# The mask of the first five attention pairs as a small matmul, with other due times for the planner

## The chip, the cores and the metric

One core of a Trainium2 chip runs the whole kernel. The metric is the device time of one execution in microseconds (us). Five engines work side by side: TensorE (PE; its weight loads have a row of their own, PEld), VectorE (DVE), ScalarE (ACT), GpSimd (POOL) and SyncE (SP), whose queue issues all of this kernel's transfers.

## What is computed

Block-causal attention for 4 batches, 8 heads, 576 positions and 64 channels a head, then two mixing blocks on its output:

```python
scores = scale * np.matmul(q, k.transpose(0, 1, 3, 2))
mask = pos[:, None] // 64 >= pos[None, :] // 64
scores = np.where(mask, scores, -1000000000.0)
attn = softmax(scores)                       # written out with max, exp, sum
x = np.matmul(attn, v)                       # heads side by side: 576 x 512 a batch
theta = x @ w_theta
zr, zi = x * np.cos(theta), x * np.sin(theta)
y = w_tok_r @ zr + w_tok_i @ zi              # over the 576 positions
u = x + y
x = u + np.maximum(u @ w_ch, 0.0)
u = x + low_rank_mix(x)                      # U, V of rank 32, over the positions
out = u + np.maximum(u @ w_ch1, 0.0) @ w_ch2 # 512 -> 2048 -> 512
```

Weights arrive as 64-bit floats and are decoded on the chip to a pair of 32-bit parts (high and low).

## The kernel before

The attention works on pairs of heads: 4 pairs a batch, 16 in all, numbered gp = 0 to 15. A pair has five row tiles of up to 128 positions (t = 0 to 4). `prep(gp)` loads q, k and v of a pair and scales q; `smax(gp, t)` makes the scores of a row tile and their softmax; `norm(gp)` takes the reciprocals of the row sums; `trans(gp, t, hh)` transposes the probabilities; `av(gp, part)` multiplies them by v (tiles oA and oB). One pair's `smax` calls are interleaved with the `trans` and `av` calls of the pair before.

In `smax` the two heads sit in the lower and upper 64 partitions of q and k, and write to the two banks of a score tile s. For t = 0 two blocks are made at once, one of 128 and one of 256 columns (the second is read by t = 1); t = 2 and 3 make 384 and 512 columns. Within a row tile the upper 64 rows must not see the last 64 columns. A DVE memset writes NEG = -1.0e30 there, behind the matmuls and ahead of the DVE reduction that takes the maximum (nm). ACT then takes the exponentials (P). t = 4 needs no mask.

`load_weight` brings one weight in two halves (raw_th, raw_tok, raw_ch) and `decode` turns them into high and low parts: two ACT activations and two DVE operations a half (da_th, da_tok, da_ch), then a rounding (on POOL, DVE or ACT) and a subtraction (on POOL or DVE). For each batch follow `theta` (five tiles), `sines` (once the five are there: one ACT table load, then the sines), `product` (five tiles), `mix_r`, `mix_i`, `chan`, `lowrank` and `expand`. The feed-forward (m and acc) runs over all batches at the end and begins earlier in gaps.

The order of the instructions is written by a planner in the kernel file. Each call is queued with a due time; the due times come from `CFG`, in units in which the four pairs of a batch take L = 60. Batch b's theta tiles are due from (b + 1) x 60 on, spread over T; the sines one after T, the products spread over P, then R and I for the mixing, twice X for the low-rank part. The weights of theta are due between d0 and d1 (as parts of 60), the first five token weights between d1 and d2, the others up to `dec`. `Line.run` lays out all operations by these due times, engine by engine, with a cost formula for each instruction. `Line.plan` repeats that four times with the latest possible starts of the layout before as the new due times, and keeps the round that it sees end first. Operations marked as `either` may go to any of two or three engines. `keep_warm` puts stand-in transposes (t<-ident, rb<-ident) into TensorE's planned gaps in the early part. All planned instructions are issued from one line, 1195.

Of the kernel before, what the change touches and what calls it, by code (L numbers as in the profile page):

```python
# [12 lines left out]
F32 = mybir.dt.float32  # L13
# [11 lines left out]
P = 128  # L25
# [10 lines left out]
NEG = -1.0e30  # L36
# [7 lines left out]


TC = {'schedule_with_timeline_sim': True}
CFG = dict(L=60., d0=0., d1=0.7, d2=1.0, dec=1.8, T=8.4, P=10., R=25.74, I=29.568, X=7., m0=4., m1=70., w1=1., w2=2., w3=0.2, wx=24., po=0.5)
ENG = dict(qs="p", pt00="a", pt01="d", pt20="a", pt21="d", pt30="a", pt31="d", pt40="a", pt41="d", pt5="d", oA="d", oB="d", nrm="p", xd="p", xh="p", zh="p", zl="p", uh="a", ul="p", sh="p", sl="p", dl="p", dh="a", os="p")
NR = 15
PA = 2  # L50
# [18 lines left out]
ROUNDS = 4  # L69
PATIENCE = 0.0  # L70
WARM = 140e3


class Op:
# [453 lines left out]
def build(tc, ctx, qT, kT, v, w_theta, wtokT, w_ch, U, V, w1, w2, outT):  # L528
    nc = tc.nc
    w_theta, wtokT, w_ch, U, V, w1, w2 = [a.bitcast(U32) for a in (w_theta, wtokT, w_ch, U, V, w1, w2)]  # L530
# [38 lines left out]
    const = ctx.enter_context(tc.tile_pool(name="const", bufs=1))  # L569
# [13 lines left out]
    warm = const.tile([P, 1], F32, name="warm")  # L583
    nc.scalar.activation(out=warm, in_=halfpi, func=AF.Exp)

    real = nc
    nc = line = Line(nc)
    pools = {"wk": ctx.enter_context(tc.tile_pool(name="wk", bufs=1)),
# [69 lines left out]
    def smax(gp, t):  # L658
        n = "%d_%d" % divmod(gp, NC4)
        if gp not in sx:  # L660
            sx[gp] = {a: line.tile([P, 9], F32, a, f"{a}{n}") for a in ("nm", "sm", "rs")}
            ptiles[gp] = {}
        x = sx[gp]
        nm, sm = x["nm"], x["sm"]
        q, k = qk[gp]
        if t != 1:
            x["s"] = line.tile([P, 2, 512], F32, "s0" if gp < 4 else "ss", f"s{n}_{t}", PSUM)
        s = x["s"]
        i = 2 * t
        if t < 4:  # L670
            W = P * (t + 1)
            src = s[:, :, 256:512] if t == 1 else s[:, :, :W]
            if t == 0:
                both = [(s[:, :, :P], 0, P), (s[:, :, 256:512], P, 2 * P)]
            elif t > 1:
                both = [(src, t * P, W)]
            if t != 1:
                line.together(lambda: [nc.tensor.matmul(y[:, hh], q[64 * hh:64 * hh + 64, c0:c0 + P],
                                                        k[64 * hh:64 * hh + 64, :w], start=True, stop=True)
                                       for y, c0, w in both for hh in range(2)])  # L680
                last = s.rearrange("p h (g c) -> p h g c", c=64)[0:64, :, 1::6] if t == 0 else src[0:64, :, W - 64:W]
                nc.vector.memset(last, NEG)
            pt = line.tile([P, 2, W], F32, f"P{t}", f"P{n}_{t}")
            nc.vector.tensor_reduce(out=nm[:, i:i + 2], in_=src, axis=AX.X, op=ALU.max, negate=True)
            for hh in range(2):
                nc.scalar.activation(out=pt[:, hh], in_=src[:, hh], func=AF.Exp, bias=nm[:, i + hh:i + hh + 1],
                                     scale=1.0, accum_out=sm[:, i + hh:i + hh + 1])
        else:
            for g in range(2):
                nc.tensor.matmul(s[:, g, :SH], q[:, 512:640], k[:, g * SH:(g + 1) * SH], start=True, stop=True)  # L690
            pt = line.tile([P, S], F32, "P4", f"P{n}_4")
            src = s[:, :, :SH]
            nc.vector.tensor_reduce(out=nm[:, i:i + 1], in_=src, axis=AX.XY, op=ALU.max, negate=True)
            nc.scalar.activation(out=pt.rearrange("p (g c) -> p g c", g=2), in_=src, func=AF.Exp,
                                 bias=nm[:, i:i + 1], scale=1.0, accum_out=sm[:, i:i + 1])
        ptiles[gp][t] = pt
# [252 lines left out]
    def at_time(t, fn, *args):  # L949
        units.append((t, len(units), fn, args))  # L950

    def spread(t0, t1, calls):
        for i, c in enumerate(calls):
            at_time(t0 + (t1 - t0) * i / len(calls), *c)
# [8 lines left out]
    def pair_calls(gp):  # L963
        calls = []
        for x in ORD.split():
            if x[0] == "S" and gp + 1 < NP:
                calls.append((smax, gp + 1, int(x[1])))
            elif x == "N" and gp + 1 < NP:
                calls.append((norm, gp + 1))
            elif x == "L" and gp + 2 < NP:  # L970
                calls.append((prep, gp + 2))
            elif x[0] == "T":
                calls.append((trans, gp, int(x[1])) + ((int(x[2]),) if len(x) > 2 else ()))
            elif x[0] == "A":
                calls.append((av, gp, int(x[1])))
        return calls

    for c in ((prep, 0),) + tuple((smax, 0, t) for t in range(NS)) + ((norm, 0), (prep, 1)):
        at_time(-1.0, *c)
    L = CFG["L"]  # L980
    for gp in range(NP):
        spread(gp * L / NC4, (gp + 1) * L / NC4, pair_calls(gp))
    d0, d1, d2, d3 = [L * CFG[x] for x in ("d0", "d1", "d2", "dec")]
    spread(d0, d1, [(load_weight, "th", w_theta, k, DM) for k in range(NC4)])
# [3 lines left out]
    for b in range(B):  # L988
        t0 = (b + 1) * L
        if b == B - 1:  # L990
            t0 += 1.0
        spread(t0, t0 + CFG["T"], [(theta, b, i) for i in range(NS)])
        t0 += CFG["T"]
        at_time(t0, sines, b)
        t0 += 1.0
        spread(t0, t0 + CFG["P"], [(product, b, i) for i in (4, 0, 1, 2, 3)])
        t0 += CFG["P"]
        spread(t0, t0 + CFG["R"], [(mix_r, b, g, d) for g in range(2) for d in range(NC4)])
# [18 lines left out]
    wx = []  # L1017
# [134 lines left out]
    def keep_warm(order):  # L1152
# [7 lines left out]
        for o in order:  # L1160
            if o.pe and o.start < WARM:
                free = [(-q[i][0], j, q[i][2]) for j, q in enumerate(homes.values()) for i in range(len(q))
# [78 lines left out]
```

## Time and profile before

| | |
|---|---|
| median of three runs | 861.77 us (859.32, 861.77, 861.82) |
| the profiled execution's own time | 861.41 us |
| its span, first to last instruction | 859.6 us |
| mean granted TensorE clock | 0.998 of full |
| busy share: PE, PEld, DVE, ACT, POOL | 98%, 80%, 48%, 44%, 31% |

The shares are means over the span. The stretches differ a lot: the first 60 us belong to the attention of batch 0 and to the weights, from about 60 to 505 us attention, mixing and the beginning of the feed-forward overlap, and from 505 us on there is only the feed-forward. A matmul's row counts its whole duration, and several may overlap; the weight loads' row is closer to how densely TensorE is fed.

### The profile page before, as it was taken

The numbers are of one execution on the slowest core, as the hardware profiler recorded it, in microseconds if no ns is written. First come the engines' busy times: TensorE is split into PE (matmuls) and PEld (weight loads), VectorE is DVE, ScalarE is ACT, GpSimd is POOL, SyncE is SP. The second block draws the span as 40 slices with busy tenths as digits, with TensorE's granted clock in tenths as the row PEclk, the third lists the DMA queues.
The fourth block names the chain that finished last, engine by engine and source line by source line (L and its number), as shares of the span: only waits on it lengthen the run. The fifth ranks groups of instructions, "written<-read, shape, count | busy, mean of one in ns | idle before, by whom it ended". The sixth has DMA issues, their size and how long they took to land.

```text
span 859.6 us, 12665 instructions
## 1 busy us (share of the span) xinstructions
PE 841.3 (98%) x4902; PEld 687.4 (80%) x4902; DVE 414.2 (48%) x793; ACT 374.4 (44%) x862; POOL 263.4 (31%) x286
## 2 busy tenths in 40 slices
PE   8999999999999999999999999999999999999998
PEld 6656688887888878988889778898888888888886
DVE  5997687467546575288756951512111311120112
ACT  6987977676556765359344641211101111111010
POOL 3546356534143431566253350404000500010000
PEclk9999999999999999999999999999999999999999
DMA  6652231110201102053423440402000100010001
GB/s 216 189 181 75 97 99 56 44 43 32 100 16 46 44 3 71 23 186 111 136 92 123 158 137 0 152 4 74 1 0 1 50 1 0 1 50 1 0 1 49
DMA packets 41595, 57.18 MB, mean 67 GB/s; under 512 B 4672, under 2 KB 25664, under 8 KB 41536
## 3 DMA queue, kind: packets, MB, share of 16 engines
q1 hardware_dynamic: 41536, 56.39, 20.1%
q8 instruction: 38, 0.62, 0.3%
q14 instruction: 21, 0.17, 0.1%
HBM read 46.94 MB, written 9.44 MB: 66 GB/s over the span
## 4 chain that ended last, share of the span: by engine, by line
PE 84%; DVE 6%; ACT 5%; DMA 2%; issue 1%; POOL 1%; SPq 0%; ACTq 0%; DVEq 0%; POOLq 0%
PE acc L1195 22%; PE m L1195 21%; PE y L1195 12%; PE c L1195 5%; PE th L1195 5%; PE s L1195 5%; PE t L1195 5%; PE oB L1195 4%; DVE d_w L1195 2%; DMA raw_w<-w 1%; ACT P L1195 1%; PE oA L1195 1%; PE xp L1195 1%; PE G L1195 1%; DMA raw_th<-w_theta 1%
## 5 line engine op out<-in xcount | busy, mean ns | idle before, releaser
L1195 PE MATMUL acc<-hh,w 128*128 128x512 f32 (+1 forms) x900 | 205.4, 373 | 1.1 <-ACT hh L1195 0.4
L1195 PE MATMUL m<-us,w 128*128 128x512 f32 (+1 forms) x900 | 203.1, 372 | 0.3 <-DVE w L1195 0.3
L1195 PEld LDWEIGHTS acc<-hh,w 128*128 128x128 f32 x900 | 156.6, 188 | 34.1 <-DVE o L1195 1.4
L1195 PEld LDWEIGHTS m<-us,w 128*128 128x128 f32 x900 | 156.8, 188 | 31.1 <-DVE w L1195 0.8
L1195 DVE SCALAR_TENSOR_TENSOR hh<-m,hh 128x512 fp32r<-128x512 f32 (+1 forms) x80 | 51.0, 637 | 266.2 <-ACT hh L1195 266.2
L1195 ACT ACTIVATE hh<-m 128x512 fp32r<-128x512 f32 (+1 forms) x80 | 44.4, 555 | 293.0 <-PE m L1195 288.0
L1195 PE MATMUL y<-wtok,zh 128*128 128x288 f32 x576 | 119.9, 301 | 0.1
L1195 PEld LDWEIGHTS y<-wtok,zh 128*128 128x128 f32 x576 | 92.6, 188 | 5.3 <-DVE xT L1195 2.4
L1195 ACT ACTIVATE P<-s,nm 128x128 f32<-128x128 f32 (+2 forms) x144 | 78.9, 552 | 40.8 <-DVE nm L1195 33.3
L1195 PE MATMUL y<-wtok,zl 128*128 128x288 f32 x288 | 85.0, 297 | 0.1
L1195 PE MATMUL t<-ident,P 128*128 128x128 f32 x400 | 64.5, 280 | 4.9 <-ACT PTB L1195 1.4
L1195 DVE TENSOR_REDUCE nm<-s 128x2 f32<-128x256 f32 (+4 forms) x80 | 64.3, 804 | 6.8 <-PE s L1195 3.4
L1195 PE MATMUL s<-k,q 64*128 64x128 f32 (+4 forms) x320 | 65.8, 459 | 0.0
L1195 PEld LDWEIGHTS t<-ident,P 128*128 128x128 f32 x400 | 47.9, 142 | 18.4 <-ACT P L1195 2.5
L1195 PE MATMUL c<-u,wch 128*128 128x288 f32 x384 | 60.3, 302 | 0.8 <-DVE u L1195 0.8
L1195 PEld LDWEIGHTS c<-u,wch 128*128 128x128 f32 x384 | 53.8, 188 | 5.5 <-issue 1.7
L1195 POOL TENSOR_TENSOR o<-us,us 128x512 f32<-128x512 f32 x16 | 20.7, 1320 | 115.4 <-DMA outT<-o 85.5
L1195 PEld LDWEIGHTS y<-wtok,zl 128*128 128x128 f32 x288 | 53.9, 188 | 1.7 <-POOL zl L1195 0.6
L1195 DVE TENSOR_TENSOR xT<-y,xT 128x288 f32<-128x288 f32 x64 | 29.0, 454 | 50.3 <-PE y L1195 49.6
L1195 PE MATMUL th<-wth,xh 128*128 128x512 f32 x160 | 51.9, 404 | 0.2 <-ACT xh L1195 0.2
L1195 ACT COPY PTB<-t 128x384 f32<-128x384 f32 (+3 forms) x68 | 30.4, 460 | 34.7 <-PE t L1195 33.6
L1195 POOL TENSOR_TENSOR zl<-f,zh 128x512 fp32r<-128x512 f32 x18 | 23.0, 1292 | 64.2 <-PE y L1195 61.4
(163 smaller groups left out, 1141.9 us busy)
## 6 DMA issues: line engine op xcount, KB each, us to landing
raw_w<-w SPq DMA_DIRECT2D x32, 512.0 KB, 4.0
raw_tok<-wtokT SPq DMA_DIRECT2D x18, 288.0 KB, 3.3
q<-qT SPq DMA_DIRECT2D x16, 320.0 KB, 2.9
vr<-v SPq DMA_DIRECT2D x16, 320.0 KB, 3.3
k<-kT SPq DMA_DIRECT2D x16, 288.0 KB, 3.3
u3d<-xT SPq DMA_DIRECT2D x16, 288.0 KB, 2.2
outT<-o SPq DMA_DIRECT2D x16, 256.0 KB, 2.1
raw_th<-w_theta SPq DMA_DIRECT2D x8, 256.0 KB, 5.4
```

Of the source, the lines that this page charges most:

```text
L1195: fn(*[place(x) for x in args], **{k: place(x) for k, x in kw.items()})
```

## The change

For gp < NMASK = 5, `smax` issues no memset. Instead, each group of score matmuls is followed by a mask product for each head into the last 64 columns of its block: a constant tile mrow, whose first row in each half has ones in columns 0 to 63, times a constant tile mneg, whose first row in each half is NEG. It is accumulated onto the scores (start=False). Six DVE memsets at the beginning build the two constants. Pairs 5 to 15 keep the memset. In `CFG` five due-time settings differ: d1 0.7 to 0.84, T 8.4 to 13.68, P 10 to 13.88, X 7 to 2.61 and m1 70 to 72.64.

```diff
-CFG = dict(L=60., d0=0., d1=0.7, d2=1.0, dec=1.8, T=8.4, P=10., R=25.74, I=29.568, X=7., m0=4., m1=70., w1=1., w2=2., w3=0.2, wx=24., po=0.5)
+CFG = dict(L=60., d0=0., d1=0.84, d2=1.0, dec=1.8, T=13.68, P=13.88, R=25.74, I=29.568, X=2.61, m0=4., m1=72.64, w1=1., w2=2., w3=0.2, wx=24., po=0.5)
...
+NMASK = 5
...
+    mrow, mneg = const.tile([P, P], F32, name="mrow"), const.tile([P, 64], F32, name="mneg")
+    for t_, f_, v_ in ((mrow, 64, 1.0), (mneg, 64, NEG)):
+        nc.vector.memset(t_, 0.0)
+        for h_ in range(2):
+            nc.vector.memset(t_[64 * h_:64 * h_ + 1, 0:f_], v_)
...
-                line.together(lambda: [nc.tensor.matmul(y[:, hh], q[64 * hh:64 * hh + 64, c0:c0 + P],
-                                                        k[64 * hh:64 * hh + 64, :w], start=True, stop=True)
-                                       for y, c0, w in both for hh in range(2)])
+                line.together(lambda: [nc.tensor.matmul(y[:, hh, w - 64:w], mrow[64 * hh:64 * hh + 64],
+                                                        mneg[64 * hh:64 * hh + 64], start=False, stop=True) if masks else
+                                       nc.tensor.matmul(y[:, hh], q[64 * hh:64 * hh + 64, c0:c0 + P],
+                                                        k[64 * hh:64 * hh + 64, :w], start=True, stop=gp >= NMASK)
+                                       for y, c0, w in both for masks in range(1 + (gp < NMASK)) for hh in range(2)])
+            if t != 1 and gp >= NMASK:
                 last = s.rearrange("p h (g c) -> p h g c", c=64)[0:64, :, 1::6] if t == 0 else src[0:64, :, W - 64:W]
                 nc.vector.memset(last, NEG)
```

## Rows read from the trace of the kernel before

**Rows 1.** The page: span, engines' busy time, chain that ended last by engine

```profile
span 859.6 us, 12665 instructions
PE 841.3 (98%) x4902; PEld 687.4 (80%) x4902; DVE 414.2 (48%) x793; ACT 374.4 (44%) x862; POOL 263.4 (31%) x286
PE 84%; DVE 6%; ACT 5%; DMA 2%; issue 1%; POOL 1%; SPq 0%; ACTq 0%; DVEq 0%; POOLq 0%
```

**Rows 2.** Busy time of each engine by stretches (the columns are named first)

```profile
core 0: us, PE busy (x) PEld busy (x) DVE busy (x) ACT busy (x) POOL busy (x), PEclk, DMA share, GB/s
...
10.00:60.00 50.00, 46.18 (x333) 30.63 (x335) 47.06 (x109) 48.62 (x149) 23.07 (x25) 1.00 0.56 175
60.00:100.00 40.00, 38.74 (x249) 26.84 (x245) 29.28 (x66) 31.09 (x84) 22.17 (x26) 1.00 0.34 108
100.00:115.00 15.00, 13.64 (x96) 10.76 (x97) 12.88 (x28) 14.32 (x28) 8.11 (x8) 0.89 0.23 74
...
505.00:859.60 354.60, 349.26 (x1693) 289.92 (x1691) 68.40 (x110) 45.54 (x83) 41.75 (x36) 1.00 0.08 25
```

**Rows 3.** Timeline of TensorE and ACT between theta and y (start, us, what)

```profile
96.70 0.39 PE L1195 MATMUL th<-wth,xl 128*128 128x512 f32 x1
...
102.80 1.28 ACT L1195 ACT_TABLE_LOAD   x1
...
108.88 1.58 PE L1195 MATMUL t<-ident 128*128 128x128 f32 x13
...
110.99 0.60 PE L1195 MATMUL t<-ident 128*128 128x128 f32 x4
...
112.07 0.82 PE L1195 MATMUL t<-ident 128*128 128x128 f32 x6
112.80 0.50 PE L1195 MATMUL y<-wtok,zh 128*128 128x288 f32 x2
```

**Rows 4.** Memsets of scores to 62 us, grouped, and the fifteenth (timeline)

```profile
L1195 DVE MEMSET s<- 64x128 f32 x10 | 1.6, 165 | 0.7 <-PE s L1195 0.5
...
L1195 DVE MEMSET s<- 64x256 f32 x5 | 1.4, 272 | 5.3 <-PE s L1195 5.2
...
54.68 0.17 DVE L1195 MEMSET s<- 64x128 f32 x1
```

**Rows 5.** Score matmuls: all (page), a first tile's (timeline), a form's sum

```profile
L1195 PE MATMUL s<-k,q 64*128 64x128 f32 (+4 forms) x320 | 65.8, 459 | 0.0
...
14.01 0.52 PEld L1195 LDWEIGHTS s<-k,q 64*128 64x128 f32 x8 [0.17 <-issue]
14.02 0.93 PE L1195 MATMUL s<-k,q 64*128 64x128 f32 x8
...
L1195 PE MATMUL s<-k,q 64*128 64x128 f32 x24 | 3.3, 351 | 0.0
```

**Rows 6.** Timeline of the first pair's first tile (in brackets: idle before, releaser)

```profile
4.61 1.79 PEld L1195 LDWEIGHTS s<-k,q 64*128 64x128 f32 x12 [0.40 <-POOL q L1195]
4.61 3.76 PE L1195 MATMUL s<-k,q 64*128 64x128 f32 x16
6.39 0.27 DVE L1195 MEMSET s<- 64x256 f32 x1 [5.19 <-PE s L1195]
...
6.70 0.42 DVE L1195 TENSOR_REDUCE nm<-s 128x2 f32<-128x256 f32 x1
7.23 0.37 ACT L1195 ACTIVATE P<-s,nm 128x128 f32<-128x128 f32 x1 [5.00 <-DVE nm L1195]
```

**Rows 7.** Decoding of token weights to 62 us, grouped (busy us, mean ns)

```profile
L1195 ACT ACTIVATE raw_tok<-raw_tok 128x288 uint32<-128x288 uint32 x12 | 5.8, 483 | 0.0
L1195 ACT ACTIVATE da_tok<-raw_tok 128x288 f32<-128x288 f32 x12 | 5.8, 482 | 0.0
...
L1195 DVE SCALAR_TENSOR_TENSOR da_tok<-da_tok,raw_tok 128x288 uint32<-128x288 uint32 x11 | 5.6, 513 | 0.0
...
L1195 DVE SCALAR_TENSOR_TENSOR da_tok<-raw_tok,da_tok 128x288 uint32<-128x288 uint32 x10 | 4.5, 446 | 0.0
```

## The prediction

> **What bounds the kernel now.** I read the page first: part 1 for the engines, part 4 for the chain that ended last [rows 1]. TensorE carries 84% of that chain and its matmul row is busy 98% of the span, so the kernel reads as bound by TensorE throughout. The table by stretches, read next, splits that up [rows 2]. From 505 us to the end (354.6 us, the dense feed-forward) DVE is busy 68.4 us and ACT 45.5 us: nothing but TensorE counts there, and the change touches no instruction of it. From 10 to 60 us it is the other way round. ACT is busy 48.6 us of 50 and DVE 47.1 us of 50, while TensorE's weight loads take 30.6 us of 50. Its matmul row still says 46.2 us, but matmuls overlap in it: 24 of the first tile with a mean of 351 ns cover 3.3 us, not 8.4 [rows 5]. In this lead-in the attention of batch 0 and the decoding of weights fill ACT and DVE; whatever is taken off both shortens it. From 60 to 100 us ACT has 8.9 us free and DVE 10.7 us. From 100 to 115 us TensorE's weight loads fall short again (10.8 of 15 us) and the granted clock averages 0.89. The timeline shows why [rows 3]: batch 0's last theta matmul starts at 96.70 us, the table load before its sines only at 102.80 us, and the first mixing matmul of y at 112.80 us. Between them stand short attention products and 23 stand-in transposes (13, 4 and 6).
>
> The execution profiled has a time of 861.41 us around a span of 859.6 us; the median of the three runs is 861.77 us, 0.36 us above it. The sum is made against 861.41, and about 0.3% (2.6 us) is what a measurement of this kernel can tell from no change.
>
> **Part 1, the memsets that go.** Each of the first five pairs loses one memset of 64x256 at 272 ns and two of 64x128 at 165 ns: in all 1.4 + 1.6 = 3.0 us of DVE [rows 4]. The last of the fifteen starts at 54.68 us, so all lie in the lead-in [rows 4]. DVE is nearly full there, but so is ACT, which loses nothing by this edit. Copies may go to either engine, so the planner can hand DVE part of ACT's. If they balance, the stretch gets half of it, 1.5 us; the bounds are 0 (ACT alone sets the pace) and 3.0 (DVE alone). I take -1.5, since the two engines' idle times in the lead-in (1.4 and 2.9 us of 50) are near each other.
>
> **Part 2, the matmuls that come.** A pair gets 4 mask products at t = 0 and 2 each at t = 2 and 3. The trace shows two matmul instructions for each fp32 product: 320 score matmuls are 16 pairs of 10 products [rows 5]. So a pair gets 16 instructions and five pairs 80. No row has a 64-row matmul of 64 columns. The nearest are the 8 score matmuls of a first tile, half of 128 and half of 256 columns: their weight loads follow each other in 0.52 us, and the eight are through in 0.93 us [rows 5]. That is 65 to 116 ns each, and 5.2 to 9.3 us for 80. Between 10 and 60 us the cover is TensorE's slack, 50 - 30.6 = 19.4 us by its weight loads. So I cost them at nothing there; without that cover all 5.2 to 9.3 us would be paid. On the way from scores to maximum they replace a step: memset to reduction takes 0.31 us (6.39 to 6.70), against 4 or 8 mask matmuls of 65 to 116 ns (0.26 to 0.93 us). Later pairs have other work on DVE and ACT meanwhile.
>
> The exception is the start. Pair 0's scores begin at 4.61 us, its memset waits for TensorE until 6.39 us, and ACT waits 5.00 us for the first exponentials [rows 6]. Eight masks more, at the pace of those first matmuls, less the 0.31 us saved, come at once on the path: between 0 (the loads overlap) and 1.2 us (8 more at (6.39 - 4.61)/8 = 0.22 us, less 0.31 and rounded down). I take +0.5. The six memsets of the constant tiles come before that, while DVE waits 5.19 us [rows 6]; even six at the 272 ns of the dearest memset in the trace are 1.6 us, so they cost nothing. Without that wait they would cost at most those 1.6 us.
>
> **Part 3, the due times.** They give the planner's first round its order; later rounds replace them by latest starts and the best round is kept. d1 from 0.7 to 0.84 moves batch 0's first five token weights from due times 42, 45.6, 49.2, 52.8, 56.4 to 50.4, 52.3, 54.2, 56.2, 58.1. The first three move by 8.4, 6.7 and 5.0 units, the others by 3.4 and 1.7. The trace shows six token weights through ACT before 62 us: 12 halves, two activations each, 11.6 us in all [rows 7]. But their first use is at 112.80 us [rows 3]. So they fill the very engines that bound the lead-in, long before they are needed. One weight costs ACT 2 x (0.482 + 0.483) = 1.93 us, and DVE 2 x (0.513 + 0.446) = 1.92 us [rows 7]. Behind 60 us there is room on both (8.9 and 10.7 us, rows of the same table [rows 2]). If two of the three weights that move most go past 60 us, the lead-in is 2 x 1.93 = 3.9 us shorter; none gives 0 and three give 5.8. I take -3.8, just under two. Their two DMAs each move along on SP's queue: at 0.56 of the DMA engines' time in the lead-in and 0.34 after it [rows 2] they have room in both places. A decode that slips too far would be late at 112.80 us for y; two weights need 3.9 us of ACT by then, and 8.9 are free.
>
> T from 8.4 to 13.68 and P from 10 to 13.88 spread theta and the products of every batch; X from 7 to 2.61 draws the low-rank part together; m1 only moves the feed-forward's target. They add and remove no instruction. All in all a batch's stages last 89.1 instead of 88.7 units. I cost them at 0, between -4.2 us (the 15 - 10.8 us that weight loads leave free from 100 to 115 us, all filled) and +4.2 us (as much again, if sines and products come later).
>
> **Sum.** -1.5 + 0.5 - 3.8 + 0 = -4.8 us: 861.41 - 4.8 = 856.6 us. TensorE is the limit behind the lead-in, so what the lead-in saves arrives at the end if its order still feeds it.
>
> **The rivals.**
> *More than that.* The hole from 100 to 115 us closes as well, by filling it with delayed decodes and attention. For it: only ACT is full there (14.3 of 15 us), and TensorE has both gaps and a lower clock [rows 2]. Against it: a longer T lets theta end later, not sooner. Price: 4.2 us more, 852.4 us.
> *No change.* Later rounds overwrite the due times, so the token weights stay where they are, and ACT's 48.6 of 50 us hold the lead-in whatever DVE sheds. What is left is between -1.5 and +0.5: about 861 us. For it: ACT's idle is half of DVE's.
> *Slower: theta's spread lengthens the hole.* Place: 96.70 to 112.80 us, where y waits for the sines of all five theta tiles. Due times there move by 5.28 (theta) and 3.88 (products) units. If the first mixing matmul comes later by half of the 9.2 units, taken as microseconds, and attention can't fill it, 4.6 us are added and, at worst, nothing of part 3 is gained: 861.4 - 1.0 + 4.6 = 865.0 us. It decides as soon as the hole grows by more than the lead-in shrinks, 4.8 us if both weights move.
> *Slower: TensorE is the bound already in the lead-in.* If its matmul row (46.2 of 50 us) is right and not its weight loads, 3.8 us are free for 5.2 to 9.3 us: 1.4 to 5.5 us are added, which gives 862.8 to 866.9 us if nothing else is gained. Against it: where TensorE really is full, weight loads take 289.9 of 354.6 us (82%), not 61% [rows 2].
> The Trainium skill bears on this last rival from both sides. Its page "Trainium Kernel Development and Optimization", section "Performance Expectations", says that matmul busy time misleads and that weight-load time is the one to read; the 61% against 82% of this trace fit that, and by it the masks are covered. Its page "TensorE: Matmul & The Clock Gate", section "LDWEIGHTS (loading the stationary operand)", says that a load's time follows its columns, 128/1.2 = 107 ns here, and not its rows. By that 80 loads would be an estimated 8.5 us, uncovered a loss that outweighs this forecast. The first-tile row has 65 ns between loads, since heads sit in different row halves.
>
> **How the numbers follow.** Forecast 0.42 (856.6, its own range 854 to 859); more 0.19 (849 to 854); no change 0.21 (859 to 864); slower by theta 0.13 and by TensorE 0.05 (864 to 867). Faster is then 0.42 + 0.19 = 0.61, same 0.21, slower 0.18. The low end takes the bounds -3.0 + 0 - 5.8 - 4.2 = -13.0, or 848.4, which needs all at once; 849 leaves that out. The high end cuts most of the slower cases at 864. Predicted: 856.6.
>
> **What would show it.** In the trace after: no DVE memset of scores before 60 us; 80 more TensorE instructions on the score tiles; the fifth pair's output product ends some 4 us earlier than now; ten rather than twelve token halves decoded before 60 us, if only one weight moves, eight if two; the reduction of pair 0 starts about 0.5 us later than 6.70 us. The prediction is wrong if y starts later than 112.8 us, if ACT stays as full for as long as now, or if the gain of the lead-in is gone by 505 us because another order leaves TensorE waiting later.

## The result, and the profile after

The changed kernel takes 865.87 us (median of five runs, 864.29 to 866.70) against 861.48 us before (five runs, 859.32 to 861.82). The ratio is 1.0056, with a 95% interval of 1.0045 to 1.0067: slower by some 4.8 us (4.4 by the medians), where 4.8 us less were forecast, and outside the range of 849 to 864 us. The profiled execution took 865.93 us, and its page answers to [rows 1]:

```profile
span 864.1 us, 12719 instructions
PE 842.3 (97%) x4943; PEld 696.5 (81%) x4943; DVE 418.4 (48%) x803; ACT 375.0 (43%) x863; POOL 245.1 (28%) x266
PE 86%; DVE 6%; ACT 4%; issue 1%; DMA 1%; POOL 1%; SPq 0%; DVEq 0%; POOLq 0%; ACTq 0%
```

By these totals little happened: no engine is busier by more than 1.3% of its time, and POOL is busy 7% less. TensorE has 41 matmul instructions more, which are 80 for the masks less 39 stand-ins (43 against 82 before). The table by stretches, with the columns of [rows 2], does show something:

```profile
10.00:60.00 50.00, 42.16 (x321) 29.81 (x319) 45.71 (x93) 44.93 (x139) 13.97 (x14) 0.97 0.53 169
60.00:100.00 40.00, 39.81 (x270) 27.78 (x268) 28.93 (x60) 32.67 (x89) 19.36 (x24) 1.00 0.31 95
100.00:115.00 15.00, 11.07 (x71) 8.16 (x68) 13.73 (x31) 13.88 (x29) 7.44 (x9) 0.94 0.39 130
505.00:864.10 359.10, 354.15 (x1706) 294.87 (x1704) 67.64 (x110) 44.20 (x80) 38.67 (x32) 0.99 0.08 25
```

In the lead-in ACT now does 44.9 instead of 48.6 us of work in the same 50 us, DVE 45.7 instead of 47.1, and POOL 14.0 instead of 23.1: the engines that were full before are not full, so something keeps them waiting. The end of theta, the table load and the first mixing matmul [rows 3] come 7.9, 8.1 and 10.3 us later, and a y later than 112.8 us was one of the prediction's own signs of being wrong:

```profile
104.61 0.39 PE L1205 MATMUL th<-wth,xl 128*128 128x512 f32 x1
...
110.90 1.28 ACT L1205 ACT_TABLE_LOAD   x1
...
123.13 0.51 PE L1205 MATMUL y<-wtok,zh 128*128 128x288 f32 x2
```

Most of that is regained later, as I read it by feed-forward work that fills the gaps; 4.5 us of span are left. The first tile, in the timeline, answers to [rows 6]:

```profile
4.80 0.80 PE L1205 MATMUL s<-k,q 64*128 64x128 f32 x4 [0.19 <-DMA k<-kT]
...
5.36 0.56 PE L1205 MATMUL s<-mneg,mrow 64*128 64x64 f32 x4
...
6.63 0.56 PE L1205 MATMUL s<-mneg,mrow 64*128 64x64 f32 x4
...
7.24 0.42 DVE L1205 TENSOR_REDUCE nm<-s 128x2 f32<-128x256 f32 x1 [5.09 <-PE s L1205]
7.70 0.37 ACT L1205 ACTIVATE P<-s,nm 128x128 f32<-128x128 f32 x1 [5.47 <-DVE nm L1205]
```

The reduction starts 0.54 us later than before, the first exponential 0.47. The first scores themselves start 0.19 us later (4.80 against 4.61), behind a DMA of k. The groups up to 62 us (busy us, mean ns) answer to [rows 4] and [rows 7]:

```profile
L1205 PE MATMUL s<-mneg,mrow 64*128 64x64 f32 x76 | 7.2, 269 | 0.0
...
L1205 DVE SCALAR_TENSOR_TENSOR da_tok<-da_tok,raw_tok 128x288 uint32<-128x288 uint32 x12 | 6.9, 590 | 0.0
...
L1205 ACT ACTIVATE raw_tok<-raw_tok 128x288 uint32<-128x288 uint32 x12 | 5.7, 475 | 0.0
```

There is no memset of scores among them, there are mask products in their place (76 of the 80; the last starts at 63.53 us), and twelve halves of token weights are decoded, as many as before. None has moved out of the lead-in.

What holds the engines up is in the groups of waits from 10 to 72 us (engine, what waited, for what: us in all, times, longest):

```profile
POOL wtok L1205 <- DVE da_tok L1205: 21.1, 4, 10.5
POOL wth L1205 <- DVE da_th L1205: 18.2, 1, 18.2
ACT P L1205 <- DVE nm L1205: 3.6, 5, 1.5
...
PEld s L1205 <- ACT P L1205: 2.7, 4, 1.9
...
DVE PTA L1205 <- PE t L1205: 2.4, 1, 2.4
```

POOL stands for 18.2 us in front of one theta weight, which is the next instruction in its order; its share of subtractions and scalings is on DVE and ACT, or comes later. The timeline around 30 us shows what may be one result:

```profile
28.56 2.71 POOL L1205 TENSOR_TENSOR wth<-da_th,wth 128x512 fp32r<-128x512 f32 x2
...
30.07 2.35 DVE L1205 TENSOR_TENSOR wth<-da_th,wth 128x512 fp32r<-128x512 f32 x2
...
33.46 0.47 ACT L1205 ACTIVATE P<-s,nm 128x256 f32<-128x256 f32 x1 [1.48 <-DVE nm L1205]
...
35.05 1.33 PE L1205 MATMUL s<-k,q 128*128 128x288 f32 x2 [1.69 <-ACT P L1205]
```

POOL, late, and DVE subtract theta weights at the same time. DVE's maxima (nm) come behind that, ACT waits 1.48 us for one, and TensorE 1.69 us for ACT. That the order is worse is a reading so far. Whether masks, due times or the planner made it so, the runs had to tell.

### The profile page after: what moved, and what is told of

The parts are those of the page before. It is cut to its first block, busy times and chain, and to the rows that moved or that the text cites. A ratio compares the mean times of both kernels' runs of the same rounds, so it can differ in the third digit from the quotient of the medians.

```text
span 864.1 us, 12719 instructions
## 1 busy us (share of the span) xinstructions
PE 842.3 (97%) x4943; PEld 696.5 (81%) x4943; DVE 418.4 (48%) x803; ACT 375.0 (43%) x863; POOL 245.1 (28%) x266
## 4 chain that ended last, share of the span: by engine, by line
PE 86%; DVE 6%; ACT 4%; issue 1%; DMA 1%; POOL 1%; SPq 0%; DVEq 0%; POOLq 0%; ACTq 0%
PE acc L1205 23%; PE m L1205 23%; PE y L1205 11%; PE c L1205 6%; PE th L1205 6%; PE s L1205 5%; PE t L1205 4%; PE oB L1205 3%; ACT P L1205 1%; PE oA L1205 1%; DVE nm L1205 1%; PE G L1205 1%; PE xp L1205 1%; PE h L1205 1%; PE xq L1205 1%
## 5 line engine op out<-in xcount | busy, mean ns | idle before, releaser
L1205 PEld LDWEIGHTS acc<-hh,w 128*128 128x128 f32 x900 | 159.2, 191 | 31.9 <-DVE o L1205 0.6
L1205 ACT ACTIVATE P<-s,nm 128x256 f32<-128x256 f32 (+3 forms) x144 | 78.7, 550 | 38.7 <-DVE nm L1205 35.2
L1205 PE MATMUL s<-k,q 64*128 64x128 f32 (+4 forms) x320 | 70.3, 473 | 2.2 <-ACT P L1205 2.0
L1205 PEld LDWEIGHTS s<-k,q 64*128 64x128 f32 (+1 forms) x320 | 31.9, 195 | 13.4 <-issue 6.9
L1205 ACT COPY PTB<-t 128x256 f32<-128x256 f32 (+3 forms) x66 | 28.7, 454 | 30.1 <-PE t L1205 29.6
```

The costliest lines, as they stand in the source:

```text
L1205: fn(*[place(x) for x in args], **{k: place(x) for k, x in kw.items()})
```

## The experiments

All runs have five rounds beside the kernel before on the same chip; its median there was 860.3 to 860.9 us. Most kernels use a switch that separates what the planner counts from what is issued: PLANNED names the pairs whose mask products enter the layout, MASKED those whose products are issued. Here scores(masked) returns the products of a group, with the masks or without, and line.calls takes their instructions without planning them. Without a change of PLANNED, CFG or a price, the order of all other instructions stays word for word that of the kernel it is taken from; the traces list the same instructions in the same order on TensorE, DVE, ACT and POOL. All these kernels issue the six memsets of the constant tiles, used or not.

```diff
-NMASK = 5
+PLANNED, MASKED = range(5), range(5)
...
+                group = line.together(lambda: scores(gp in PLANNED)).ways[PE_]
+                group.call = line.calls(lambda: scores(gp in MASKED))
...
+                if gp not in PLANNED:
+                    way = memset().ways[DVE_]
+                    if gp in MASKED:
+                        way.call = []
+                    memset = None
...
+            if memset and gp not in MASKED:
+                top.ways[DVE_].call = line.calls(memset) + top.ways[DVE_].call
```

**One part of the change alone.** First, both halves: masks planned with the old due times, and new due times with all memsets.

```diff
+PLANNED, MASKED = range(5), range(5)    # masks_replanned, with the old CFG
+PLANNED, MASKED = (), ()                # times_only, with the new CFG
```

> Masks for the first five pairs, due times as before; the planner lays everything out anew. Theory A (the loss comes from the order that the new due times give, the masks cost nearly nothing): within 1.5 us of the kernel before, 860 to 863 us. Theory B (the masks themselves cost their 80 x 42 ns on TensorE, 3.4 us, and more at the start): 864 to 867 us.

> The five new due times, every pair keeps its memset. Theory A: 864 to 867 us, as slow as the changed kernel. Theory B: no more than 862.5 us.

Measured: masks_replanned 863.87 us, ratio 1.0039 (1.0027 to 1.0051); times_only 859.15 us, ratio 0.9984 (0.9974 to 0.9993). The first lies between the two theories and near B, the second in theory B's range. The loss is with the masks. Not with the due times: they alone even gain 1.4 us by the ratio and 1.7 by the medians, and this is the fastest kernel found here, faster than both kernels of the case.

**The price of the products, and of the order.** Next the masks in the order of the kernel before, in place of the memsets, and the memsets in the order of the changed kernel, directly in front of the reductions.

```diff
+PLANNED, MASKED = (), range(5)          # masks_old_order, with the old CFG
+PLANNED, MASKED = range(5), ()          # memsets_new_order, with the new CFG
```

> The order of the kernel before is kept instruction for instruction; only the fifteen memsets are taken out and the 80 mask matmuls put behind the score matmuls that they belong to. This is the price of the masks without any new order. Theory A: 860.5 to 862.5 us. Theory B: 864 to 867 us. My prediction's part 1 and 2 together said -1.0 us.

> The order of the changed kernel is kept; the 80 mask matmuls are taken out and each memset stands right in front of its reduction. Theory A: 864.5 to 866.5 us. Theory B: 861 to 863 us.

Measured: masks_old_order 863.46 us, 1.0032 (1.0020 to 1.0044); memsets_new_order 869.77 us, 1.0103 (1.0090 to 1.0116). So in an order that is otherwise the same, issuing the masks costs 2.6 us although 15 memsets are gone; that is between the two theories. In the order of the changed kernel memsets in the masks' place cost 3.9 us more than the masks, above what either theory gave. Why they are so dear there no run shows; that order was laid out without them.

Why a product that TensorE should have had room for costs time is seen side by side. TensorE in the kernel before, behind the first tile of pair 1 (start, us):

```profile
14.02 0.93 PE L1195 MATMUL s<-k,q 64*128 64x128 f32 x8
14.87 1.86 PE L1195 MATMUL rb<-ident 128*128 128x128 f32 x15
16.66 0.92 PE L1195 MATMUL s<-k,q 64*128 64x384 f32 x4
17.50 1.09 PE L1195 MATMUL rb<-ident 128*128 128x128 f32 x8
18.53 1.13 PE L1195 MATMUL s<-k,q 64*128 64x512 f32 x4
```

and in masks_old_order:

```profile
14.61 0.49 PE L1224 MATMUL s<-k,q 64*128 64x128 f32 x4
14.94 0.34 PE L1224 MATMUL s<-mneg,mrow 64*128 64x64 f32 x4
15.11 0.66 PE L1224 MATMUL s<-k,q 64*128 64x256 f32 x4
15.60 0.33 PE L1224 MATMUL s<-mneg,mrow 64*128 64x64 f32 x4
15.86 1.86 PE L1224 MATMUL rb<-ident 128*128 128x128 f32 x15
17.65 0.92 PE L1224 MATMUL s<-k,q 64*128 64x384 f32 x4
```

From the first of four masks to the next scores it is 0.17 us (14.94, 15.11), 42 ns a mask. What stands behind them on TensorE starts later by about as much: the group of 384 columns was 16.66 - 14.02 = 2.64 us behind the first scores and is now 17.65 - 14.61 = 3.04 us. That is 0.40 us more, where two groups of masks at 0.17 us are 0.34. Part of what is pushed here are stand-ins, which the order fixes by number, but the transposes and row sums (t, rb) of later pairs are pushed too. Their readers stand at the head of the queues of DVE and ACT and wait for them. Groups of waits of the kernel before, 10 to 60 us:

```profile
DVE rbs L1195 <- PE rb L1195: 1.4, 2, 0.9
...
DVE PTA L1195 <- PE t L1195: 0.9, 1, 0.9
ACT PTB L1195 <- PE t L1195: 0.6, 2, 0.3
DVE PTB L1195 <- PE t L1195: 0.6, 2, 0.4
```

and of masks_old_order, 10 to 63 us:

```profile
DVE rbs L1224 <- PE rb L1224: 3.1, 2, 1.6
DVE PTB L1224 <- PE t L1224: 2.3, 5, 0.7
...
DVE PTA L1224 <- PE t L1224: 2.3, 3, 1.1
ACT PTB L1224 <- PE t L1224: 1.4, 4, 0.6
```

Two stretches of masks_old_order, with the columns of [rows 2]:

```profile
10.00:60.00 50.00, 45.97 (x372) 33.41 (x371) 41.09 (x90) 46.13 (x142) 23.05 (x25) 1.00 0.54 168
...
100.00:115.00 15.00, 12.64 (x98) 9.33 (x96) 12.62 (x28) 14.97 (x31) 8.07 (x9) 1.00 0.31 101
```

DVE waits 7.7 instead of 2.9 us for transposes and row sums, and does 41.1 us of work in the 50 instead of 47.1 (of the 6.0 us, up to 3.0 are the memsets that are gone). Setting the starts of like DVE and ACT instructions of the two traces against each other shows how it adds up: 0.6 us late behind pair 0's start, 1.3 at 24 us, 2.5 at 33 to 37, 3.0 at 46 and 3.3 from 55 to 100 us. A pair's 16 masks at 42 ns are 0.67 us, five pairs 3.4. The last theta matmul is 3.3 us late, the table load 3.35 and the first y 2.3:

```profile
100.03 0.39 PE L1224 MATMUL th<-wth,xl 128*128 128x512 f32 x1
...
106.15 1.28 ACT L1224 ACT_TABLE_LOAD   x1
115.10 0.50 PE L1224 MATMUL y<-wtok,zh 128*128 128x288 f32 x2
```

The microsecond regained before y goes with the granted clock from 100 to 115 us, 1.00 here and 0.89 in [rows 2]. It is no gain of the masks: two runs below without masks, d1_only and no_mask_old_order, issue the same order at a clock of 1.00 there, and their traces regain 1.0 us at the same place. Before it, at 100 us, they stand 0.7 us late and 0.2 us early against the kernel before, so a single trace tells the 3.3 us to no better than that.

**Masks with the new due times, doubled, and gone.** Three controls: masks in the order of times_only, each mask twice in the order of before, and neither mask nor memset in the order of before. The last leaves the first five pairs unmasked.

```diff
+PLANNED, MASKED = (), range(5)          # masks_in_times_order, new CFG; masks_doubled_old_order, old CFG
...
+                group.call = line.calls(lambda: scores(2 * (gp in MASKED)))     # masks_doubled_old_order
...
+                    if gp < 5:                                                  # no_mask_old_order, old CFG
+                        way.call = []
```

> The order that the new due times give without masks (the kernel of times_only), with the fifteen memsets replaced in place by the 80 mask matmuls. If masks and due times simply add up (times_only 859.15, masks in the old order +2.6): 861 to 862.5 us. Then the changed kernel's 865.87 us is some 4 us more than the sum, and they come from the order that the planner writes when it counts the masks in. If instead masks and new due times collide by themselves: 864.5 to 866.5 us.

> The old order with every mask matmul issued twice (the mask is added twice; the result of the softmax does not change). Theory C (each mask group stands in TensorE's queue ahead of transposes that DVE and ACT wait for, 0.7 us a pair): another 2.5 to 3.5 us, 866 to 867 us. Theory D (the 2.6 us of the masks come from the start of pair 0 and from the clock, not from their time on TensorE): 863 to 864 us.

> The old order with neither memset nor mask for the first five pairs (their mask is left out). This prices my part 1 alone: 3.0 us of DVE taken away. If DVE's load sets the pace of the lead-in: 858 to 859.4 us. If the memsets were hidden: 860.4 to 861.4 us.

Measured: masks_in_times_order 861.85 us, 1.0015 (1.0007 to 1.0024), which is 0.0031 over times_only; masks_doubled_old_order 868.38 us, 1.0086 (1.0071 to 1.0101); no_mask_old_order 860.18 us, 0.9997 (0.9989 to 1.0006). The first set of masks costs 0.0032 to 0.0035 of the time, the second 0.0054, and the memsets nothing that can be told from zero. Theory D is out. The second set costs 4.9 us by the medians, more than theory C's 2.5 to 3.5 us: with doubled masks the eight of pair 1's first group reach from 16.47 to 16.87 us in the trace, 50 ns each, and those of pair 0 from 5.27 to 6.02 us, 94 ns each, so the price of 42 ns does not hold for any number of masks. Products and due times add up as long as the order is not planned with the masks. The changed kernel is 4 us above that sum.

**Each due time alone,** all with the memsets (parts of the CFG line):

```diff
-d1=0.7
+d1=0.84                        # d1_only
...
-T=8.4, P=10.
+T=13.68, P=13.88               # T_and_P_only
...
-X=7., m1=70.
+X=2.61, m1=72.64               # X_and_m1_only
```

> Only d1 = 0.84, everything else as before, planned anew. My part 3 put its whole gain here: by it 856.5 to 858 us. The rival, that later rounds of the planner overwrite the due times: 860 to 862 us. times_only gave 859.15 us with all five settings.

> Memsets for every pair, only T = 13.68 and P = 13.88 new. times_only gained 1.75 us over the kernel before and d1 alone nothing, so the gain is here or in X and m1. If a wider spread of theta and products brings it: 858.5 to 859.5 us. My rival that a longer T lengthens the hole between theta and y: 862 to 865 us. If it is in X and m1: 860 to 861 us.

> Memsets for every pair, only X = 2.61 and m1 = 72.64 new. If the gain of times_only is here: 858.5 to 859.5 us; else 860 to 861.5 us. The prediction had these two at nothing.

Measured: d1_only 860.72 us, 0.9999 (0.9990 to 1.0007); T_and_P_only 864.21 us, 1.0048 (1.0032 to 1.0064); X_and_m1_only 862.12 us, 1.0020 (1.0011 to 1.0029). Their sum is +0.0067, all five together gave -0.0016. They don't add, so none of the three is the price of its due time. In the trace of d1_only these four engines have the same instructions in the same order as in the kernel before: this due time changed nothing in the final order. T_and_P_only lies in the range of the rival of the longer hole, but its hole is that of times_only, 5 us faster: from the last theta matmul to the first y it is 95.80 to 113.72 us in the one and 95.55 to 113.49 in the other, 17.9 us in both. X_and_m1_only lies above both of its ranges.

**A right price for the products.** The planner counts a mask product (two instructions) at 160.5 ns, and the traces show 2 x 42 = 85. Counted so, with new and old due times:

```diff
+                group.cost -= (160.5 - 85.0) * 2 * len(both) * (gp in PLANNED)
```

> The changed kernel with one number of the planner changed: a mask product counts 85 ns of TensorE, as the trace shows (two matmuls of 42 ns), instead of 160.5 ns. The same instructions are issued, in the order that comes out. Theory E (the planner's price for the masks leads it to the bad order of the lead-in): 861 to 863 us, like masks_in_times_order. Theory F (any layout that counts the masks in and follows these due times comes out badly, whatever the price): 864.5 to 867 us.

> The same price of 85 ns with the old due times. masks_replanned gave 863.87 us and masks_old_order 863.46. Theory E: 862.5 to 864 us, no worse than the old order with masks. Theory F says nothing here; if it comes out above 865, orders scatter by some us from small causes.

Measured: masks_priced_right 863.42 us, 1.0037 (1.0025 to 1.0049); masks_priced_right_old_times 863.40 us, 1.0038 (1.0025 to 1.0050). With the new due times it is some 2 us better than the changed kernel, between the two theories, and still slower than before. With the old due times the price changes nothing (1.0038 against 1.0039).

**The order without masks.** The changed kernel's order and the rightly priced one, with neither masks nor memsets in the first five pairs, so unmasked there:

```diff
+PLANNED, MASKED = range(5), ()          # both, new CFG; neither_priced_right with the price above
...
+            if memset and gp not in MASKED and gp >= 5:
```

> The planner lays out the changed kernel, mask products counted, with the new due times; then neither mask products nor memsets are issued for the first five pairs, so their upper 64 rows are not masked. Theory G: the mask products keep their own price of about 2.6 us in any order, and the order that the planner writes when it counts them costs the other 4.0 us against the order with the new due times alone. Then 865.9 - 2.6 = 863.3 us. Theory H: in an order that is planned with them the mask products lie in gaps and are hidden, and the whole 6.7 us against 859.15 are the order's. Then 865.9 us, as the changed kernel.

> As masks_priced_right (new due times, planned with mask products at 85 ns a product), but neither mask products nor memsets are issued for the first five pairs. Theory G: 863.4 - 2.6 = 860.8 us, near the kernel before, so that order is as good as the old one and only the products' own price is left. Theory H: 863.4 us, the products are hidden there and the order alone is 2.5 to 3 us worse than the kernel before.

Measured: neither_new_order 864.40 us, 1.0034 (1.0021 to 1.0047); neither_priced_right 863.39 us, 1.0027 (1.0018 to 1.0036). The first time lies between the theories, the second is that of theory H. In the changed kernel's order the masks cost 1.0056 - 1.0034 = 0.0022 (0.0005 to 0.0039 from the two intervals), or 1.9 us, and the order alone 2.9. In the rightly priced order issuing them costs 0.0010, with an interval from the two of -0.0005 to 0.0025: less than the 0.0032 of the old order, and not to be told from nothing. So a layout that knows the products may hide a part of them; the intervals leave that open. What the two runs do show is that the rest of such a layout is worse than the old one, by 0.0027 to 0.0034, with no mask in it at all.

**How much an order is worth.** The last four neither add nor remove work. The planner counts each score group of the first five pairs 4 or 12 ns dearer (twice that for the first group), with the old and with the new due times, all with memsets:

```diff
+PLANNED, MASKED = (), ()                # price_* with the old CFG, times_plus_* with the new
...
+                group.cost += 4 * len(both) * (gp < 5)      # 12 in the *_12ns
```

> The kernel before with its memsets and old due times, but the planner counts each group of score matmuls of the first five pairs 4 ns (8 ns for the first group) dearer, a change far below what any duration repeats to. No instruction is added or removed; only the order may change. Theory I: the planner's layouts scatter, so that such a nudge alone moves the time by more than 1.5 us either way; then the order's share in the changed kernel's loss says little of the masks. Theory J: without a real change of load the order stays as good, and the time is within 1 us of the kernel before.

> As price_plus_4ns with 12 ns (24 for the first group). Theory I: a time that differs from the kernel before and from price_plus_4ns by more than 1.5 us in either direction, at least for one of them. Theory J: within 1 us of the kernel before.

> As times_only (new due times, all memsets, 859.15 us), with score groups of the first five pairs 4 ns dearer for the planner. Theory I: the gain of 1.6 us is one draw of a scatter and is lost or turned, 861 to 864 us. Theory J: the new due times are worth their gain in any nearby layout: 858.5 to 860 us.

> As times_plus_4ns with 12 ns. Theory I: 861 to 864 us, or at least over 1.5 us from times_only. Theory J: 858.5 to 860 us.

Measured: price_plus_4ns 864.26 us, 1.0039 (1.0027 to 1.0051); price_plus_12ns 874.06 us, 1.0162 (1.0149 to 1.0176); times_plus_4ns 861.28 us, 1.0009 (1.0000 to 1.0018); times_plus_12ns 861.17 us, 1.0009 (1.0001 to 1.0018). A nudge of 4 ns costs 3.4 us, one of 12 ns 13 us, and the gain of the new due times is lost with either. Theory I holds. What changes is the order, the engine of operations that may go to several, and the number of stand-ins (82 before; 113 and 100 in the two with the old due times). The six constant memsets are not what changes it, since d1_only has them too and keeps the old order. Much of what the 12 ns cost lies far from the edited pairs: from 400 to 440 us TensorE's weight loads fill 25.75 us in price_plus_12ns (first line) against 33.68 in the kernel before (second):

```profile
400.00:440.00 40.00, 32.93 (x174) 25.75 (x173) 31.07 (x50) 24.66 (x43) 14.11 (x16) 1.00 0.41 130
```

```profile
400.00:440.00 40.00, 39.84 (x239) 33.68 (x238) 27.50 (x46) 18.42 (x34) 16.43 (x15) 1.00 0.36 120
```

## Why the prediction was wrong

**The account of the loss.** In ratios, 1.0056 is 0.0034 for the order that the planner wrote and 0.0022 for issuing the masks: 2.9 and 1.9 us. Both terms are shown by runs, the second with a wide interval. The forecast was off by 9.6 us, from -4.8 to +4.8. Set against its terms that is 3.8 us for the decodes that did not move (part 3), 2.9 us for a new order, which the sum had at nothing, 1.5 us for the memsets (part 1) and 1.4 us for the masks (part 2, 1.9 instead of +0.5). That the order is worse *because* of the masks is not shown: orders that changed for other reasons lie between 0.9984 and 1.0162, and 0.0034 is an ordinary place among them. Equally, times_only's 0.9984 is a good draw and not a proven worth of its due times, since its two neighbours have 1.0009.

**A cause that no run tested.** The order's share may come by way of the granted clock, which is on record for every execution. Of the kernel before, about fifty executions at a mean clock of 1.000 have a median of 860.0 us, and as many at 0.996 to 0.998 one of 861.1 us. Over all twenty kernels, compared within the executions of each, 0.001 less goes with 0.4 us more. The changed kernel's five executions have 0.988 to 0.994 and neither_new_order's seven 0.990 to 0.994, against 0.999 on the mean before. By that slope an estimated 3 us of the changed kernel's loss, and most of the 2.9 us of its order, go with the clock; none of masks_old_order's 2.6 us do (0.998 to 1.000). It is not shown which way this works, since waits may lower the clock and cost time as well. Nor is a low clock enough or needed for a place among the kernels: times_only is the fastest at 0.992 to 0.996, and masks_priced_right has 1.0037 at 0.997 to 1.000.

**Part 1 (-1.5) failed by its size.** Without memsets and masks the old order gave -0.4 us with an interval around zero. The memsets were as good as hidden. That DVE and ACT were both nearly full was right, but memset time taken off one of them did not shorten the lead-in. What bound it instead, by my reading the chain through their queues and TensorE's, is argued and not shown.

**Part 2 failed in its mechanism.** "Between 10 and 60 us the cover is TensorE's slack ... so I cost them at nothing there" took a busy share for cover. The slack of 19.4 us exists, but it is not where the masks are issued. They stand in front of transposes and row sums whose readers are the next instructions of DVE and ACT, so most of their 80 x 42 ns = 3.4 us is passed on: +2.6 us in the old order, +1.9 in the changed one. The Trainium skill, page "Trainium Kernel Development and Optimization", section "Performance Expectations", which I had read as saying that the masks are covered, gives weight-load share as a measure of distance to the roofline. It promises no cover at a given place, and the 61% of this trace went with a price of 2.6 us. The bounds of 65 to 116 ns for an instruction were too high for most masks, 42 ns by starts; the 65 ns counted the last load of the row to its end. The +0.5 us for the start came out at its size (0.54 for the reduction, 0.47 for the exponential), but in part by luck. In masks_old_order, with the same eight masks, the reduction starts at 6.57 us and the exponential at 7.03, earlier than the 6.70 and 7.23 before. In the changed kernel the first scores were late, and four masks of pair 0 take up to 0.32 us instead of 0.17. The upper bound of that term is also added up wrongly: 8 x 0.22 - 0.31 is 1.5 us and not 1.2. The constant tiles' memsets were hidden, as the reduction still waits 5.09 us for TensorE.

**Part 3 (-3.8) failed in its mechanism, and is the largest miss.** It took a later due time for a later decode. No token weight left the lead-in, twelve halves are still decoded there, and d1 alone is worth nothing (0.9999) and leaves the order as it was. The rival "no change" foresaw that and gave a reason, that later rounds overwrite the first due times; the identical order fits it. What the rounds do to the layout under the other settings was the missing part. The due times are a seed to the planner rather than a plan.

**T, P, X, m1 (0, between -4.2 and +4.2)**: +3.9 and +1.8 us by the medians in the two runs, -1.7 all five together. The bounds held, but the reasons given for them are not borne out: nudges that touch none of these stages move the time as much, and the two runs don't add up to the whole. That a new order might cost time by itself is what was put at nothing here.

**The rivals.** "TensorE is the bound already in the lead-in" named 862.8 to 866.9 us and comes nearest for the masks, by luck, since its mechanism is another: 1.4 to 5.5 us for a TensorE that has no room, where a frozen order with room by its weight loads (33.4 of 50 us) cost 2.6. It was given 0.05. "Theta's spread lengthens the hole" saw the gap from the last theta matmul to y, and it did grow, from 16.1 to 18.5 us (the 16.1 hold the lower clock; the same order has 15.0 us at 1.00). Its 865.0 us are near the measured time, yet times_only has 17.9 us there and was still faster. Not considered at all was that a replanned order is by itself a risk of 3 us and more: the largest term of the result.

**What stays open.** Which decision of the planner sent POOL into its 18.2 us wait, and whether that is what costs the 2.9 us, was read from the trace and not tried. neither_new_order has the same wait (17.3 us) without masks, which fits. But neither_priced_right has no wait of POOL above 4.8 us between 10 and 72 us, starts y at 112.57 us, as early as the kernel before, and its order is still 0.0027 slower. So an order can be nearly as bad with neither the long wait nor a late y. How much of the 2.6 us in the old order is due to its fixed stand-ins is open too.

## What to carry to other kernels

A low busy share is no cover: a new instruction delays what stands behind it on its engine, so look up what that is and who reads it, and multiply the issue time by the count (here 80 x 42 ns = 3.4 us, of which 2.6 arrived). When an order comes from a planner, measure its scatter first, with nudges of a few ns that neither add nor remove work. An edit worth less than that scatter has to be tested in a frozen order, and a good draw should not be credited to the setting that led to it.

## What the hardware showed that was not expected

- A group of four mask matmuls of 64 rows by 64 columns in fp32 moves the next scores back by 0.17 us, 42 ns each. With each mask issued twice it is 50 ns each, and at the start (pair 0) 94 ns. The memsets that they replace are 165 and 272 ns, but on an engine where they cost nothing that could be told from zero.
- A DVE subtraction of two SBUF tensors stretches beside POOL's. The pair at 30.07 us in the changed kernel takes 2.35 us, 1.75 for the one beside POOL and 0.68 for the other, and a single one of a token weight 1.96 us at 53.03 us, where POOL is busy throughout. The Trainium skill, page "SBUF — State Buffer", section "Who interferes with whom", says that a DVE instruction with two inputs in SBUF contends with a GpSimd instruction that reads SBUF, and that only one of them has the port at a time. The rows at 28.56 and 30.07 us agree: the two engines overlap until 31.27 us, during the first of the two subtractions only.
- The granted clock goes to 0.50, the lower of its two levels (1.2 GHz), in three stretches of the changed kernel: for 3.4 us from 34.7 us, near the end of the 1.69 us wait above; for 6.8 us from 113.2 us, in the hole before y; and for 6.8 us from 550.1 us, behind small products and waits of the low-rank part that the kernel before has as well, at full clock. Nor does a thin stretch settle it: from 100 to 115 us masks_old_order keeps 1.00 with 9.33 us of weight loads, and the kernel before has 0.89 with 10.76 [rows 2].
